# Four stores instead of two for the last 64 tokens of each sequence, in a gated recurrence with soft MoE slots

## The chip, the cores and the metric

The kernel runs on one core of a Trainium2 chip. The metric is the device time of one execution in microseconds; the median of the runs counts.

## The reference, cut to what matters

```python
B, S, D = 4, 5056, 256
# 1. a gated recurrence over each sequence
f = lower_bound + (1 - lower_bound) * sigmoid(f_logit)
for t in range(S):
    h = f[:, t] * h + (1 - f[:, t]) * x[:, t]
    y[:, t] = h
x = y.reshape(B * S, D)                    # 20224 tokens
# 2. soft MoE: 8 experts with 4 slots each, 32 slots
logits = x @ phi
d = softmax(logits, over all tokens)
slot_input = (d.T @ x).reshape(8, 4, D)
for e in range(8):
    slot_out[e] = relu(slot_input[e] @ w1[e]) @ w2[e]
c = softmax(logits, over the 32 slots)
out = c @ slot_out.reshape(32, D)          # 20224 x 256, float32
```

Every token's output needs the slots' outputs, and these need every token. So no output row can be written before the whole input has been read and the experts are done.

## The kernel before, in words

The kernel has three stages on one core. The order on each engine is written out by hand.

Until about 118 us it reads `x` and `f_logit` in groups of 512 tokens of a sequence, forms the gates, turns them to channels by TensorE, runs the recurrence as a scan on VectorE (L319), and takes logits and exponentials from its result. The exponentials of all tokens stay in SBUF (`etall`; for the last L = 64 tokens of each sequence a copy in `left`). The weights of the experts come in meanwhile by GpSimd's DMA queue (`load_w`). Then follows the small expert stage (L605 to L749), in which the outputs of the slots are made.

The last stage begins near 143.5 us and writes 20.7 MB. For a tile of 128 rows, TensorE multiplies the exponentials with the slots' outputs, and VectorE (`by_vector`, L756) or ScalarE (`by_scalar`, L760) scales the rows from PSUM into a tile of the pool `osb`, which holds three buffers for each of the names `ob` and `oc`. SP (SyncE) issues every store, in this order:

- `early` (L747): two stores of 128 KB, the first rows of sequence 3.
- `pieces` (L796): five stores of 256 or 512 KB, the rest of the first 2048 tokens of sequence 3.
- `couple(end, 0)` and `couple(end, 1)` (L828): four stores of 896 KB, the tokens 4096 to 4991 of all four sequences.
- `rest` (L845): the last 64 tokens of all sequences. Its tile `ob` has on its 128 partitions 64 tokens x 2 sequences (partition 2t + u is token t of sequence 2j + u) and the two pairs j of sequences side by side. For each pair one store goes from 128 partitions with 1 KB each to `dst[64 tokens, 2 sequences]`, so every row is a run of 1 KB in DRAM.
- `whole` (L813): one store of 2 MB.
- three calls of `couple` (L828): six stores of 2 MB.

SP takes its instructions in order. Before a store it waits for the engines that fill the tile, and for the completion semaphore that this store will use. The program has eight such semaphores for SP's DMAs and uses them in turn, so that each store waits for the landing of the DMA eight places before it. After the last store SP waits for the landing of all (L882).

Of the kernel before, what the change touches and what calls it, by code (L numbers as in the profile page):

```python
# [18 lines left out]
def kernel(  # L19
# [10 lines left out]
    nc = tc.nc  # L30
    B, S, D = x.shape
# [17 lines left out]
    def used(g):  # L49
        return first(g + 1) - first(g) if g < n_grp - 1 else G  # L50
# [6 lines left out]
    L = used(odd) - P * R3  # L57
# [110 lines left out]
    with tc.tile_pool(name="sp2", bufs=3) as sp2, \  # L168
# [85 lines left out]
        def to_channels(n, ps, t, rest):  # L254
            t = t.bitcast(F32)
            if n // B == odd:
                flat = ps.rearrange("c p r -> c (p r)")
                sides = ident_f.rearrange("p (t u) -> p u t", u=2)
                v = flat[:, ds(0, P * R3)].rearrange("c (p r) -> c p r", r=R3)
                k = P * R3 - n % 2 * L  # L260
                nc.tensor.matmul(flat[:, ds(k, P)], rest.bitcast(F32), sides,
                                 is_transpose=True, start=True, stop=True)
                for r in range(R3):
                    nc.tensor.transpose(v[:, :, r], t[:, r], ident_f)
                return
            for r in range(R):
                nc.tensor.transpose(ps[:, :, r], t[:, r], ident_f)  # L267
# [337 lines left out]
    with tc.tile_pool(name="ew", bufs=1) as ew, \  # L605
# [36 lines left out]
        for q in range(E // Q):  # L642
# [4 lines left out]
            if q == 0:  # L647
                nc.tensor.matmul(cs_ps, rep2, cs1, start=True, stop=True)
            k = Q if q == 0 else Q - 1
# [4 lines left out]
            dst = hid[:, :, q * Q, ds(s0, SPE)]  # L654
            dst = bass.AP(tensor=dst.tensor, offset=dst.offset,
                          ap=[list(dst.ap[0]), [(E - 1) * NS, FC], [NS + SPE, k], [1, SPE]])
# [55 lines left out]
        for i in range(len(blocks)):  # L712
            expert(Q + i)
            row_sums(i)
            if i < len(blocks) - 1:
                k = ds(i * wide_r, wide_r)
# [3 lines left out]
        k = len(blocks) - 1  # L720
# [32 lines left out]
    with tc.tile_pool(name="osb", bufs=3, reuse_waits="tile") as osb:  # L753

        def by_vector(ob, op, scale):
            nc.vector.tensor_tensor(ob, op, scale.broadcast_to(list(ob.shape)), ALU.mult)  # L756
# [22 lines left out]
        def bank():  # L779
            return pout.tile([P, 2, D], F32, name="op", tag="op")  # L780
# [49 lines left out]
        def rest():  # L830
            n_p = B // 2
            ob = osb.tile([P, n_p, D], F32, name="ob", tag="ob")
            dst = out.rearrange("(b t) d -> t b d", b=B)
            for j in range(n_p):
                k = ds(j * 2 * NS, 2 * NS)
                op = bank()
                nc.tensor.matmul(op.rearrange("p u d -> p (u d)"),
                                 left[k].rearrange("s t u -> s (t u)"),
                                 slot_bd[k].rearrange("s u d -> s (u d)"),
                                 start=True, stop=True, skip_group_check=True)  # L840
                nc.scalar.copy(ob[:, j], op[:, 0])
                nc.vector.tensor_tensor(ob[:, j], ob[:, j], op[:, 1], ALU.add)
            by_vector(ob, ob, rrow[:, n_grp * R - 1, ds(0, n_p)].unsqueeze(2))
            for j in range(n_p):
                nc.sync.dma_start(out=dst[ds(S - L, L), ds(2 * j, 2)], in_=ob[:, j])  # L845

        pieces(0, B - 1)
        end = len(blocks) - 1
        couple(end, 0)
        couple(end, 1)  # L850
        rest()
        whole(0, B - 2)
        for i in range(end):
# [33 lines left out]
```

## Time and profile before

| what | value |
|---|---|
| median of 3 runs | 198.1 us (197.61 to 198.96) |
| profiled execution | 197.64 us, of which the span is 195.9 us |
| PE, DVE, ACT, POOL busy, share of the span | 76%, 73%, 73%, 52% |
| HBM read and written | 58.23 MB and 20.71 MB |
| DMA packets | 14161, of them 2866 under 2 KB |
| last stage | 143.5 us to the end |

The span runs from the first to the last instruction on the core; the profiled execution's own time has 1.7 us more around it. Engine shares are averages over stages with different limits: in the last 20 us no compute engine works, and stores alone are under way. A DMA of this kernel is cut into packets, one for each row, which 16 DMA engines of the core work off, and each engine sends a mark of 4 bytes when its share of a store is done. Where a time "to landing" is given, it runs from the issue on SP to the last of these marks.

### The profile page before, as it was taken

The page shows a single profiled execution, that of the slowest core. Times are in us where ns is not written, and L with a number is a line of the kernel's source. Part 1 is how long each engine was busy: PE and PEld are TensorE (multiplying, and loading weights), DVE is VectorE, ACT ScalarE, POOL GpSimd, SP SyncE. Part 2 cuts the span into 40 slices and gives each one's busy share as a digit, 9 for nine tenths or more (in the row PEclk, how much of TensorE's full clock was granted, in tenths as well). Part 3 has the DMA queues.
Part 4 walks back from the last instruction along what each step waited for, and adds up shares of the span by engine and source line. Part 5 has one row for each costly group of instructions (what it writes and reads, how often), then busy time and mean ns, then how long its engine had stood idle before and what let it go on. Part 6 is the DMA issues. An engine that isn't in the chain of part 4 may idle for free.

```text
span 195.9 us, 3272 instructions
## 1 busy us (share of the span) xinstructions
PE 149.7 (76%) x1204; PEld 105.0 (54%) x1204; DVE 143.9 (73%) x185; ACT 142.0 (73%) x200; POOL 101.2 (52%) x78
## 2 busy tenths in 40 slices
PE   0687599977998979899797988997899999930000
PEld 0465468675776767767585856556674434300000
DVE  2669859989799999999999999543377998930000
ACT  3689686899889999999987799434089999950000
POOL 2589578774998688874969979280030000000000
PEclk9999759996999999999999999999996555555555
DMA  5999999999999999999999999999849999999994
GB/s 195 416 419 421 433 428 423 428 428 363 363 422 428 412 331 427 423 414 333 379 420 421 253 218 213 213 212 214 162 170 424 429 424 428 425 445 435 445 435 174
DMA packets 14161, 70.75 MB, mean 361 GB/s; under 512 B 1585, under 2 KB 2866, under 8 KB 10178
## 3 DMA queue, kind: packets, MB, share of 16 engines
q1 hardware_dynamic: 11520, 62.13, 76.5%
q0 software_dynamic: 2624, 8.42, 21.6%
q8 instruction: 9, 0.15, 0.3%
q14 instruction: 6, 0.05, 0.1%
q10 hardware_dynamic: 2, 0.00, 0.0%
HBM read 58.23 MB, written 20.71 MB: 403 GB/s over the span
## 4 chain that ended last, share of the span: by engine, by line
PE 34%; DMA 24%; DVE 13%; POOL 9%; issue 5%; ACT 4%; ACTq 0%; SPq 0%; POOLq 0%
DMA x_t<-in_x_dram 14%; DVE h L319 10%; DMA w_t<-in_moe_w_dram 9%; PE op L822 9%; POOL u_t L252 7%; PE hp L332 5%; PE up L273 4%; PE sp L267 4%; ACT oc L760 3%; DVE ht L351 3%; PE op L766 3%; PE slot_ps L189 2%; PE lg L365 2%; POOL w_sb L147 2%; PE slot_ps L416 1%
## 5 line engine op out<-in xcount | busy, mean ns | idle before, releaser
L252 POOL TENSOR_TENSOR u_t<-s_t,x_t 128x1024 bf16<-128x1024 bf16 (+1 forms) x39 | 82.5, 2131 | 22.6 <-ACT s_t L241 11.8
L319 DVE TENSOR_TENSOR_SCAN h<-a,h,up 128x512 bf16<-128x512 f32 (+1 forms) x72 | 86.8, 1253 | 4.5 <-PE up L273 2.2
L241 ACT ACTIVATE s_t<-f_t 128x2048 bf16<-128x2048 f32 (+2 forms) x23 | 38.3, 1668 | 4.9 <-DMA f_t<-in_f_logit_dram 4.9
L332 PE MATMUL hp<-ident_f,h 128*128 128x128 f32 (+1 forms) x160 | 29.4, 308 | 7.9 <-DVE ht L351 6.7
L332 PEld LDWEIGHTS hp<-ident_f,h 128*128 128x128 f32 (+1 forms) x160 | 23.5, 207 | 19.1 <-DVE ht L351 12.6
L267 PE MATMUL sp<-ident_f,s_t 128*128 128x128 f32 x144 | 22.1, 298 | 6.9 <-ACT s_t L241 4.6
L301 ACT ACTIVATE a<-sp,lbs 128x1024 f32<-128x1024 bf16 x24 | 25.4, 1114 | 1.1 <-PE sp L267 0.6
L760 ACT ACTIVATE oc<-op,rrow 128x256 f32<-128x256 f32 x62 | 24.5, 513 | 0.2
L822 PE MATMUL op<-slot_bd,etall 64*128 64x512 bf16 x62 | 23.3, 582 | 0.5 <-ACT oc L760 0.3
L267 PEld LDWEIGHTS sp<-ident_f,s_t 128*128 128x128 f32 x144 | 18.0, 155 | 8.7 <-ACT s_t L241 5.1
L756 DVE TENSOR_TENSOR oc<-op,rrow 128x512 f32<-128x512 f32 x31 | 19.9, 686 | 1.9 <-PE op L822 1.8
L308 ACT ACTIVATE a<-sp,lbs 128x512 f32<-128x512 bf16 (+2 forms) x22 | 17.8, 858 | 4.7 <-PE sp L267 4.3
L273 PE MATMUL up<-ident_f,u_t 64*128 64x64 f32 x192 | 17.8, 231 | 1.8 <-POOL u_t L252 1.8
L189 PE MATMUL slot_ps<-rep,ident_f 128*128 128x256 f32 x52 | 17.5, 432 | 0.0
L273 PEld LDWEIGHTS up<-ident_f,u_t 64*128 64x128 f32 x192 | 14.1, 139 | 5.6 <-POOL u_t L252 2.1
L822 PEld LDWEIGHTS <-etall 64*128 64x128 bf16 x62 | 9.1, 154 | 13.4 <-issue 7.9
L351 ACT COPY ht<-hp 128x512 f32<-128x512 f32 (+1 forms) x20 | 11.6, 582 | 5.3 <-PE hp L332 5.2
L351 DVE COPY ht<-hp 128x512 f32<-128x512 f32 (+1 forms) x20 | 13.4, 669 | 1.3 <-PE hp L332 1.3
L319 DVE TENSOR_TENSOR_SCAN h<-a,up 128x512 bf16<-128x512 f32 x8 | 9.3, 1208 | 2.5 <-ACT a L308 1.6
L365 PE MATMUL lg<-h,phi 128*32 128x512 bf16 (+1 forms) x80 | 9.8, 412 | 0.3 <-ACT et L389 0.2
L267 PE MATMUL up<-ident_f,u_t 128*128 128x128 f32 x48 | 9.4, 328 | 0.6 <-POOL u_t L252 0.6
L189 PEld LDWEIGHTS slot_ps<-rep,ident_f 128*128 128x128 f32 x52 | 8.5, 199 | 1.8 <-issue 0.8
(127 smaller groups left out, 144.1 us busy)
## 6 DMA issues: line engine op xcount, KB each, us to landing
f_t<-in_f_logit_dram SPq DMA_DIRECT2D x12, 1024.0 KB, 12.1
x_t<-in_x_dram SPq DMA_DIRECT2D x12, 1024.0 KB, 11.5
out_dram<-oc SPq DMA_DIRECT2D x6, 2048.0 KB, 13.4
w_sb<-in_moe_w_dram POOLq DMA_DIRECT2D x14, 512.0 KB, 10.3
f_t<-in_f_logit_dram SPq DMA_DIRECT2D x12, 512.0 KB, 8.4
x_t<-in_x_dram SPq DMA_DIRECT2D x12, 512.0 KB, 9.9
out_dram<-oc SPq DMA_DIRECT2D x4, 896.0 KB, 6.1
out_dram<-ob SPq DMA_DIRECT2D x1, 2048.0 KB, 9.3
```

What stands on the lines that cost most here:

```text
L189: nc.tensor.matmul(slot_bank[:, 1], ident_f, wide_rep, start=False, stop=False, skip_group_check=True)
L241: nc.scalar.activation(s_t, f_t, ACT.Sigmoid, scale=-1.0)
L252: nc.gpsimd.tensor_tensor(uts[n][:, :r], s_t[:, :r], x_t[:, :r], ALU.mult)
L267: nc.tensor.transpose(ps[:, :, r], t[:, r], ident_f)
L273: nc.tensor.transpose(v[:, :, r], t(r)[k].bitcast(F32), ident_f[k, k])
L301: nc.scalar.activation(a, sp[:, :, :, :, o], ACT.Identity, scale=nomlb[:, ds(o, 1)], bias=1.0)
L319: nc.vector.tensor_tensor_scan(h[:, :T, o], decays[n // 2, o][:, n % 2, :T], up[:, :T, o], hs[number(g - 1, b)][:, ds(used(g - 1) - 1, 1), ...
L332: nc.tensor.transpose(hp[:n_p, r], hw[:, :n_p, r], ident_f)
L351: copy(hts[g][:n_p, b].rearrange("p r d -> p (r d)").bitcast(F32), hps.pop(n)[:n_p].rearrange("p r c -> p (r c)"))
L756: nc.vector.tensor_tensor(ob, op, scale.broadcast_to(list(ob.shape)), ALU.mult)
L760: nc.scalar.activation(ob[:, i], op[:, i], ACT.Copy, scale=scale[:, i])
L822: nc.tensor.matmul(op.rearrange("p u d -> p (u d)"), ew[:, :, r], slot_bd[ds(j * 2 * NS, 2 * NS)].rearrange("s u d -> s (u d)"), start=Tru ...
```

## The change

Each of the two stores of `rest` becomes two: one of the first 60 tokens (120 partitions) and one of the last 4 tokens (8 partitions). The bytes, the tile and the places in DRAM are the same, and no other instruction changes; SP issues 4 DMAs there instead of 2, and the stores behind them take the next completion semaphores but two.

```diff
             for j in range(n_p):
-                nc.sync.dma_start(out=dst[ds(S - L, L), ds(2 * j, 2)], in_=ob[:, j])
+                for t, k in ((0, L - 4), (L - 4, 4)):
+                    nc.sync.dma_start(out=dst[ds(S - L + t, k), ds(2 * j, 2)],
+                                      in_=ob[ds(2 * t, 2 * k), j])
```

## The prediction

> **What bounds the kernel now.** I read the page's slices first, then the windows of the last 50 us, then what SP (the engine that issues every store here) waits for, then its timeline, and last the packets of single stretches. The slices (40 of 4.9 us each):
>
> ```profile
> DMA  5999999999999999999999999999849999999994
> GB/s 195 416 419 421 433 428 423 428 428 363 363 422 428 412 331 427 423 414 333 379 420 421 253 218 213 213 212 214 162 170 424 429 424 428 425 445 435 445 435 174
> ```
>
> The stores run from slice 31 (147 us) to the last one at 424 to 445 GB/s, as fast as the loads ever went. The changed stores, L845, lie in slice 32. The windows say whether a compute engine is behind that:
>
> ```profile
> 150.00:158.00 8.00, 7.97 (x29) 4.21 (x28) 6.71 (x13) 7.99 (x23) 0.00 (x0) 0.50 1.01 423
> ...
> 174.00:192.00 18.00, 0.00 (x0) 0.00 (x0) 0.00 (x0) 0.26 (x1) 0.00 (x0) 0.50 0.99 422
> ```
>
> The columns are the stretch, its length, the busy time of PE, PEld, DVE, ACT and POOL, the granted clock, the DMA share and GB/s. After 174 us nothing computes, and the DMA engines are full (0.99) for 18 us more. SP's own waits say the same:
>
> ```profile
> SPq L882 <- DMA out_dram<-oc: 18.9, 1, 18.9
> SPq L828 <- DVE oc L756: 14.8, 5, 5.0
> ```
>
> The last store is issued at 175.5 us and SP then stands 18.9 us for landings. So the end is set by bytes on the DMA engines. A change counts only if it gives the most loaded DMA engine more time, or lets the queue run dry between 145 and 193 us.
>
> Packets show that the 16 DMA engines do not end together. The stretch 193.3 to 194.2 us:
>
> ```profile
> DMA packets 13, 0.03 MB, mean 36 GB/s; under 512 B 11, under 2 KB 11, under 8 KB 11
> q1 hardware_dynamic: 13, 0.03, 9.2%
> ```
>
> Eleven are completion marks; only two are data, 16 KB each. 9.2% of 16 engines x 0.9 us is 1.32 us, so a 16 KB packet takes about 0.6 us. Nearly all engines finish their data around 193.3; two still start a packet then and end near 194.0. The two late engines decide the end, and the rest have some 0.6 us to spare.
>
> **The change, part by part.** Four stores take the place of two. Bytes stay the same, and so do the packets: dst rows are 1 KB each, 128 a store, 256 in all before and (120 + 8) x 2 = 256 after. PE, DVE, ACT and POOL run the same instructions in the same order. The tile of L845 is in no buffer that is written again, so nobody but the end waits for its landings. What moves is how the rows fall on the 16 engines, and how long SP is at it.
>
> *Rows on engines.* The price of a row comes from 144.0 to 145.3 us, when the `early` rows of 1 KB went out:
>
> ```profile
> DMA packets 276, 0.26 MB, mean 199 GB/s; under 512 B 24, under 2 KB 276, under 8 KB 276
> q1 hardware_dynamic: 276, 0.26, 59.9%
> ```
>
> 59.9% of 16 x 1.3 us is 12.5 us; over 252 data packets (and 24 small marks) that is at most 49 ns each; I take 46, as the marks take a part. Before, 256 rows on 16 engines are 16 each, 0.74 us of every engine. After, the new stores carry 120 and 8 rows. No store in this trace has such a count. The nearest rows: stores of 128 rows, which go out at the full rate of all engines (424 GB/s), and at the far end the one-row load, one data packet and its mark on a single engine:
>
> ```profile
> q10 hardware_dynamic: 2, 0.00, 0.0%
> ```
>
> Even spread is the one end: 16 or 17 rows on the busiest engine, 0 to +0.05 us. All on one engine is the other: 256 rows, (256 - 16) x 46 ns = 11.0 us more there, and the end moves by 10.4 to 11.0 as that engine has 0.6 us to spare or not. 120 rows are far nearer 128 than 1, so I take a nearly even spread, in which the 8 rows of a short store lie on a few engines: with two more rows there per pair, 4 x 46 ns = 0.18 us. If these engines are not the two late ones, their 0.6 us hides it; if one is, the end moves by 0.18. I take +0.1 us.
>
> [...]
>
> *SP.* Its timeline around the change (start, us, what):
>
> ```profile
> 153.38 2.19 SPq L845 DMA_DIRECT2D out_dram<-ob  x2
> 155.81 1.18 SPq L813 DMA_DIRECT2D out_dram<-ob  x1
> 161.25 14.29 SPq L828 DMA_DIRECT2D out_dram<-oc  x6
> ```
>
> The two old stores of L845 (ns shortest, middle, longest, and when they were issued):
>
> ```profile
> L845 SPq DMA_DIRECT2D out_dram<-ob x2: 744/1066/1389, 153.4 to 154.2; - x2
> ```
>
> Two more issues cost from 2 x (332 + 46) ns = 0.8 us (the shortest DMA issue of L828, with the gap to the next) to 2 x (1389 + 46) = 2.9 us (the longer one of L845). I take L845's middle, 1.07 + 0.05 each, 2.2 us. Behind them on SP stands the 2 MB store of whole() (L813), which moves from 155.8 to about 158.0 (bounds 156.6 and 158.7). After it come the stores of L828; the first waits for DVE (5.0 us at the longest, until 161.25), and L813 done at 158.0 + 1.18 = 159.2, or 159.9 at worst, is before that. So the six last stores keep their times, and only L813 can leave the queue dry.
>
> The DMA issues (KB each, us from issue to landing) give the queue ahead of it:
>
> ```profile
> out_dram<-ob SPq DMA_DIRECT2D x1, 2048.0 KB, 9.3
> ...
> out_dram<-early SPq DMA_DIRECT2D x2, 128.0 KB, 1.8
> out_dram<-ob SPq DMA_DIRECT2D x2, 128.0 KB, 6.1
> ```
>
> From issue to landing L813 took 9.3 us. Its own bytes need 2.097 MB / 422 GB/s = 5.0; the `early` store with an empty queue took 1.8, of which 8 rows x 46 ns = 0.4 are data, so 1.4 are fixed. 9.3 - 5.0 - 1.4 = 2.9 us of queue lay ahead of it on the late engines, and 2.9 - 0.6 = 2.3 on the others. A delay of 2.2 fits under both. At 2.9 the 14 engines run dry for 0.6 us, which is what they have to spare, and the late ones just do not. Price: 0, bounds 0 and +0.6.
>
> *Semaphores.* SP's DMAs take eight completion semaphores in turn, each waiting for the landing of the one eight before. Two more stores shift this by two: L813 now waits for the first 896 KB store (issued 148.9, landed at the least 4.3 us later by L828's row, 153.2) instead of a store of L796; the next ones wait for the other 896 KB stores, which lie ahead of the old L845 pair in the queue, and that pair had landed at 154.2 + 6.1 = 160.3, before 161.25. Cost 0; if that cover were gone, the queue left at 161.25 (L813 lands at 165.1) would pay first.
>
> *Sum.* 0.1 (rows) + 0 (SP) + 0 (semaphores). The profiled execution, 195.9 us of span in 197.64, becomes 196.0 and 197.7. It lay 0.46 under the median of the three runs, 198.1, so the median becomes 198.2.
>
> **The rivals.**
>
> *One engine carries the rows of a 60-token store* (slower). Point of decision: an engine with n rows ends (n - 16) x 46 ns later, less 0.6 of spare, so the end moves by 1% (2 us) from n = 60 to 73 on, which is 120 rows a pair on four engines or fewer. On one engine 208.5 to 209; on four, (64 - 16) x 46 ns = 2.2, less up to 0.6: 199.7 to 200.3. For it: a count that is no multiple of 16 is unseen here, and the one-row load did stay on one engine. Against: 120 rows can be dealt out as 8 each to 15.
>
> *The queue runs dry before L813* (slower, by little). If all four issues run at the slow 1.4 us and the first bytes come late, the end moves by up to 0.6: 198.7. It would need an issue of over 3 us each to make 1%.
>
> *Each store's fixed 1.4 us is paid in line.* Two more stores would add 2.8 us: 200.9. [...] Against it in the trace: five stores of L796 were issued 0.4 us apart and the window 146 to 148 us still had a DMA share of 1.07; fixed parts overlapped.
>
> *Faster.* If the engine that gets no rows of the 60-token stores is the last of the two late ones, the other one decides, about 0.1 us earlier: 198.0. [...] No mechanism here gives 1%: the bytes are the same and the last store is issued when compute is done.
>
> **How the numbers follow.** Forecast (with the 0.1 either way) 0.68; dry queue 0.10; fixed cost in line 0.05; rows on four engines 0.07; on one 0.07; clearly faster by something not seen 0.03. About 1%, 2 us, can be told from no change here. Slower by more: one engine 0.07, fixed cost 0.05, half of the four-engine case 0.04, and 0.02 for spread of the runs (197.6 to 199.0): 0.18. Faster by more: 0.03. Same: 0.79. The range must hold 198.2 with the spread of the runs, 198.7, and the four-engine case: 197.3 to 200.3. It leaves out one engine, fixed cost and part of faster, some 0.15.
>
> **What would show it.** Right: the packets under 2 KB keep their number but for the marks; DMA share stays at 0.99 or more from 146 to 193 us; L813's issue moves to 156.6 to 158.7 and its landing time falls by as much; the first L828 of the last six stays at 161.25 within its own spread; the last landing stays within 0.2 us. Wrong: after the stretch where 14 engines end, 1 KB packets or more than two late engines are left over; a slice under 400 GB/s around 159 us; or a wait of SP for a landing ahead of L813.

## The result, and the profile after

The changed kernel takes 198.73 us in the median of 20 runs (198.49 to 200.62), the kernel before 197.61 us in 20 runs of its own (197.41 to 198.96). The ratio is 1.0053, 95% interval 1.0038 to 1.0067: about 1.05 us slower (the two medians lie 1.12 us apart). That lies inside the range of the prediction and under the 1% from which on it counts a change, but it is ten times the 0.1 us of its sum. The profiled execution of the changed kernel has a span of 197.1 us in 198.83.

The page's slices of the changed kernel (4.9 us each):

```profile
DMA  5999999999999999999999999999669999999993
GB/s 203 419 421 420 427 429 424 429 426 383 353 426 426 421 318 426 422 415 343 369 420 416 232 211 213 214 214 213 124 239 430 429 370 432 429 429 429 426 426 166
```

Slice 33 (157.7 to 162.6 us) moved 370 GB/s where the kernel before had 424. SP's timeline of the changed kernel (start, us, what) shows one step that was mis-sized:

```profile
153.41 5.65 SPq L846 DMA_DIRECT2D out_dram<-ob  x4
159.17 0.37 SPq L813 DMA_DIRECT2D out_dram<-ob  x1
161.50 1.62 SPq L828 DMA_DIRECT2D out_dram<-oc  x2
```

The four stores hold SP for 5.65 us, and `whole`'s 2 MB store (L813) goes out at 159.17, 3.36 us later than before. The windows of the changed kernel (stretch, length, busy PE, PEld, DVE, ACT, POOL, clock, DMA share, GB/s):

```profile
158.00:159.00 1.00, 1.00 (x3) 0.33 (x2) 0.90 (x3) 0.99 (x4) 0.00 (x0) 0.50 0.92 307
159.00:160.00 1.00, 1.00 (x4) 0.42 (x3) 0.84 (x2) 0.99 (x3) 0.00 (x0) 0.50 0.60 185
```

The same stretches of the kernel before:

```profile
158.00:159.00 1.00, 1.00 (x4) 0.44 (x3) 1.00 (x3) 0.99 (x3) 0.00 (x0) 0.50 1.01 391
159.00:160.00 1.00, 1.00 (x4) 0.33 (x2) 0.86 (x2) 0.97 (x4) 0.00 (x0) 0.50 1.50 613
```

A packet counts where it starts, so a share can pass 1. Between 159 and 160 us the queue did run dry on most engines: at 159.8 us only 3 of the 16 have a packet under way. That would be a complete story, but it does not set the end. The packets after 194.4 us in the changed kernel:

```profile
DMA packets 2, 0.02 MB, mean 14 GB/s; under 512 B 1, under 2 KB 1, under 8 KB 1
```

One engine alone has a 16 KB packet to go when all others are done. In the packet records the other 15 end their data at 194.12 to 194.38, this one at 195.54 (before: 193.3 to 193.4, and the two late ones at 193.97 and 194.07). If the dry stretch were all, the end would be near 194.4, only 0.3 later than before. The one late engine decides, and it did not run dry there: between its last 7 KB packets it stood still for no more than 0.05 us at a time. Instead its 7 KB packets became slow. The packets that start between 159.1 and 160 us, first of the changed kernel:

```profile
DMA packets 167, 0.16 MB, mean 173 GB/s; under 512 B 27, under 2 KB 165, under 8 KB 167
```

and of the kernel before:

```profile
DMA packets 133, 0.58 MB, mean 642 GB/s; under 512 B 19, under 2 KB 103, under 8 KB 103
```

Between "under 2 KB" and "under 8 KB" lie the 7 KB packets of the stores ahead. Before, none starts after 159.1. After, two do: they took 696 and 740 ns where 272 is the rule, after one of 586. A window of 0.01 us around the start of such a packet shows its length, since a packet counts whole where it starts. The window 158.545 to 158.555 us, then 159.88 to 159.89:

```profile
q1 hardware_dynamic: 1, 0.01, 366.2%
```

```profile
q1 hardware_dynamic: 1, 0.01, 462.5%
```

366.2% of 16 engines x 0.01 us is 586 ns, and 462.5% is 740. That engine landed its share of the last 896 KB store at 160.97, against 159.58 before: 1.39 us of loss ahead of any row of the changed stores on it. Four other engines had a slow 7 KB packet, too (445 to 614 ns, from 158.33 us on), but these have time to spare.

### The profile page after: what moved, and what is told of

The parts are those of the page before. It is cut to its first block, busy times and chain, and to the rows that moved or that the text cites. A ratio compares the mean times of both kernels' runs of the same rounds, so it can differ in the third digit from the quotient of the medians.

```text
span 197.1 us, 3274 instructions
## 1 busy us (share of the span) xinstructions
PE 150.2 (76%) x1204; PEld 105.1 (53%) x1204; DVE 144.2 (73%) x185; ACT 142.3 (72%) x200; POOL 101.4 (51%) x78
## 4 chain that ended last, share of the span: by engine, by line
PE 26%; DMA 23%; DVE 15%; POOL 9%; ACT 9%; issue 5%; ACTq 0%; SPq 0%; POOLq 0%
DMA x_t<-in_x_dram 14%; DVE h L319 12%; PE op L822 9%; DMA w_t<-in_moe_w_dram 9%; POOL u_t L252 7%; ACT oc L760 3%; PE hp L332 3%; DVE ht L351 3%; PE up L273 3%; PE op L766 3%; PE sp L267 2%; ACT s_t L241 2%; POOL w_sb L147 2%; PE lg L365 1%; PE slot_ps L189 1%
## 5 line engine op out<-in xcount | busy, mean ns | idle before, releaser
L332 PE MATMUL hp<-ident_f,h 128*128 128x128 f32 (+1 forms) x160 | 29.9, 313 | 9.5 <-DVE ht L351 8.2
```

Of the source, the lines that this page charges most:

```text
L332: nc.tensor.transpose(hp[:n_p, r], hw[:, :n_p, r], ident_f)
```

## The experiments

Three theories. A: SP is late with `whole`, and the queue runs dry. B: 15 and 4 engines in place of 16 load the rows unevenly. C (formed after the first four runs): with less than 128 partitions in a store, rows leave SBUF through other engines than those that serve these partitions in the full stores, and so slow down an engine that is still at its 7 KB rows. C is a guess: no trace names the engine or the partition of a packet. "Late engine" is the last mark of the last 896 KB store, "end" the last mark of all, both from the profiled execution; each ratio is to runs of the kernel before taken beside that kernel.

| kernel | whole() issued, us | late engine, us | end, us | ratio to before (95%) |
|---|---|---|---|---|
| before | 155.81 | 159.58 | 194.54 | 1 |
| changed | 159.17 | 160.97 | 195.85 | 1.0053 (1.0038 to 1.0067) |
| e1, 32 + 32 tokens | 158.61 | 160.53 | 195.22 | 1.0016 (0.9997 to 1.0035) |
| e2, behind whole() | 155.65 | 159.43 | 195.42 | 1.0044 (1.0018 to 1.0069) |
| e3, the 60 alone | 155.87 | 160.20 | 195.23 | 1.0034 (1.0012 to 1.0056) |
| e4, 61 + 3 | 165.55 | 161.50 | 205.04 | 1.0519 (1.0484 to 1.0554) |
| e5, column halves | 158.25 | 159.50 | 194.55 | 0.9996 (0.9988 to 1.0005) |
| e6, tokens 32 to 63 alone | 155.87 | 159.63 | 194.39 | 0.9999 (0.9986 to 1.0011) |
| e7, tokens 0 to 31 alone | 155.73 | 160.20 | 194.96 | 1.0026 (1.0014 to 1.0037) |
| e8, changed again | 159.08 | 160.91 | 195.80 | 1.0056 (1.0044 to 1.0068) |
| e9, six column stores | 159.62 | 159.58 | 195.43 | 1.0038 (1.0024 to 1.0052) |
| e10, eight column stores | 161.01 | 159.69 | 196.78 | 1.0093 (1.0079 to 1.0107) |

**e1: even halves.**

```diff
-                for t, k in ((0, L - 4), (L - 4, 4)):
+                for t, k in ((0, 32), (32, 32)):
```

> Theory A (late issue): the four issues of L846 hold SP, whole()'s 2 MB store is issued 3.4 us late as in the changed kernel, and the queue runs dry near 159.3 us. Four stores of 32 tokens cost SP about as much, so A expects +0.8 to +1.2 us over the kernel before, whole() issued near 159 us and the DMA share of 159 to 160 us near 0.6. Theory B (uneven rows): the stores of 60 tokens run on 15 DMA engines and those of 4 on four, one of the late engines among them, and its 7 KB packets grow from 272 to 586 to 740 ns. With 64 rows a store on all 16 engines B expects no slow 7 KB packets, the last engine where it was before, and -0.1 to +0.3 us.

Neither theory fits. SP is as late as A says (158.61), but the medians differ by 0.48 us (198.16 against 197.68 us; the interval of the ratio, 0.9997 to 1.0035, just includes no loss) and not by 0.8 to 1.2, and the late engine again has slow 7 KB packets (533 and 853 ns) although all 16 engines share the rows, against B.

**e2: the same stores behind whole().** Here `rest` hands its stores back instead of issuing them (that part of the edit is left out below).

```diff
-        rest()
+        stores = rest()
         whole(0, B - 2)
+        stores()
```

> The same 60 and 4 token stores, issued behind whole()'s store instead of ahead of it. A: whole() is issued near 155.7 us, its bytes fill the queue while SP is at the four stores, no dry stretch, -0.2 to +0.3 us against the kernel before. B: the same rows lie on the same engines, so the four rows more on one late engine and the slow packets stay: +0.6 to +1.2 us.

`whole` goes out at 155.65, ahead of the changed stores, and the loss stays (198.45 us). That speaks against A as the cause. The slow packets moved too: now 16 KB packets of `whole` are slow, nine of them, with 684 to 1047 ns (611 is the rule), at 162.7 to 164.7 us, about when the 1 KB rows run beside them. Two of them, of 895 and 1047 ns, follow each other; 0.72 us over the rule and the 0.18 us of the added rows make 0.90, and the end moved by 0.88.

**e3: the 4-token stores left out.**

```diff
-                for t, k in ((0, L - 4), (L - 4, 4)):
+                for t, k in ((0, L - 4),):
```

> Only the two stores of 60 tokens are issued; the last 4 tokens of each sequence are left unwritten. SP has two issues as before. A: whole() is issued at 155.8 to 156.5 us, no dry stretch, -0.2 to +0.3 us. B: if the 15-engine spread makes the slow packets, they stay (+0.6 to +1.0 us); if the four-engine stores make them, they go.

SP's timeline of this kernel:

```profile
153.30 2.46 SPq L846 DMA_DIRECT2D out_dram<-ob  x2
155.87 1.29 SPq L813 DMA_DIRECT2D out_dram<-ob  x1
```

SP is as before, there is no late issue, and 0.64 us are lost (198.32 against 197.68). So the stores of 60 tokens alone make more than half of the loss, without A. The late engine is 0.62 us later at its last 896 KB mark, which is nearly the whole of it.

**e4: a prime number of tokens.**

```diff
-                for t, k in ((0, L - 4), (L - 4, 4)):
+                for t, k in ((0, L - 3), (L - 3, 3)):
```

> The split is 61 and 3 tokens. If the number of engines is the largest up to 16 that divides both 61 and 122, a 61-token store has all its 122 rows of 1 KB on one engine: 244 + 4 rows there against 16, 232 x 46 ns = 10.7 us more, less 0 to 0.7 us of spare: +10 to +10.7 us. If rows are dealt out to all engines whatever their number, +0.8 to +1.2 us as with 60 and 4.

207.93 us, 10.25 more than 197.68: the 61-token stores do run on one engine. The issues of L846 (ns shortest, middle, longest) show SP standing behind it, too:

```profile
L846 SPq DMA_DIRECT2D out_dram<-ob x4: 667/2977/5312, 153.3 to 160.3; - x4
```

The number of engines can be read from the page, because each engine that takes part in a store sends one mark: the packet records of the kernel before have 1280 marks for SP's 80 DMAs, 16 each, so the two stores of 128 rows bring 2 x 16. The line of the kernel before, of the changed kernel, of e3, of e4 and of e1:

```profile
q1 hardware_dynamic: 11520, 62.13, 76.5%
```

```profile
q1 hardware_dynamic: 11526, 62.13, 76.1%
```

```profile
q1 hardware_dynamic: 11502, 62.12, 76.4%
```

```profile
q1 hardware_dynamic: 11496, 62.13, 72.8%
```

```profile
q1 hardware_dynamic: 11552, 62.13, 76.5%
```

The 6 more of the changed kernel are 2 x (15 + 4) - 32. e3 has 18 less: 16 rows, and 2 marks, which are 2 x 15 - 32. The 24 less of e4 are 2 x (1 + 3) - 32; another split of the 4 would give the same count, but not 10.25 us. The 32 more of e1 are 4 x 16 - 32. So these runs had 16 engines for 64 and for 32 tokens, 15 for 60, 4 for 4, 3 for 3 and 1 for 61: each time the largest number up to 16 that divides the tokens. Other counts were not tried.

**e5: columns, not tokens.** Four stores again, but each with all 128 partitions.

```diff
-                for t, k in ((0, L - 4), (L - 4, 4)):
-                    nc.sync.dma_start(out=dst[ds(S - L + t, k), ds(2 * j, 2)],
-                                      in_=ob[ds(2 * t, 2 * k), j])
+                for c in range(0, D, D // 2):
+                    nc.sync.dma_start(
+                        out=dst[ds(S - L, L), ds(2 * j, 2), ds(c, D // 2)],
+                        in_=ob[:, j, ds(c, D // 2)])
```

> Four stores as in the change, but each of all 64 tokens (128 partitions) and half of the columns, 512 rows of 512 B. Theory A (late issue): SP is as long at them, whole() is issued near 158.7 us, the queue runs dry for some tenths, and the time is +0.5 to +1.1 us over the kernel before. Theory C (crossed rows): the late engine's packets get slow because, with less than 128 partitions in a store, rows go out through other engines than those that serve the same partitions in the 128-partition stores, so that two engines draw on the same part of SBUF. Here all 128 partitions are in each store: no packet of 7168 B over 400 ns near 159 us, the last engine lands its 896 KB share where it did before (159.6 us), and the time is 0 to +0.4 us, the latter for the smaller rows.

SP's timeline of e5, and its windows:

```profile
153.30 4.84 SPq L846 DMA_DIRECT2D out_dram<-ob  x4
158.25 0.67 SPq L813 DMA_DIRECT2D out_dram<-ob  x1
```

```profile
158.00:159.00 1.00, 1.00 (x4) 0.41 (x3) 1.00 (x3) 1.00 (x4) 0.00 (x0) 0.50 0.95 332
159.00:160.00 1.00, 1.00 (x3) 0.33 (x2) 0.99 (x3) 0.99 (x4) 0.00 (x0) 0.50 1.02 379
```

Four issues, `whole` 2.4 us late, twice the packets: and no loss, 197.53 against 197.58 us. No 7 KB packet in the stretch is over 400 ns. The queue runs dry here, too, but for less time: at 159.4 us only two engines have a packet under way. Splitting these stores in four by columns, each with all partitions, costs nothing.

**e6 and e7: one half of the partitions.** Both have two stores, 64 rows each, on 16 engines (by the marks of e1), and leave the other 32 tokens unwritten. The two edits are shown as one:

```diff
-                for t, k in ((0, L - 4), (L - 4, 4)):
+                for t, k in ((32, 32),):        # e6
+                for t, k in ((0, 32),):         # e7
```

> Only the tokens 32 to 63 of the last 64 are stored (partitions 64 to 127), in two stores; the other 32 tokens are left unwritten. To be read beside its twin with the tokens 0 to 31. [...] Theory B (uneven rows): both halves are spread evenly on 16 engines, so both kernels take the same time, -0.5 to 0.

> The twin: only the tokens 0 to 31 are stored (partitions 0 to 63), the other 32 are left unwritten. [...] Theory B: the same time as the twin.

SP's last wait in e6, then in e7:

```profile
SPq L884 <- DMA out_dram<-oc: 18.7, 1, 18.7
```

```profile
SPq L884 <- DMA out_dram<-oc: 19.3, 1, 19.3
```

The upper half costs nothing (197.46 us), the lower half 0.45 (198.03 against 197.58). In e7 the late engine had a 7 KB packet of 609 ns right after one of 487; in e6 two packets took 415 and 422 ns, and the late engine's mark stands at 159.63, as before. Number of stores, issues, engines and rows are the same. What differs is which partitions the rows leave from (and which tokens they are; but e5 writes all of these tokens without loss). By B the two would have taken the same time. So C is shown as far as this: these rows from partitions 0 to 63, taken by all 16 engines, slow the late engine (0.45 us lost), and those from 64 to 127 do not (197.46 against 197.58 us).

What the rows share with the late engine's packets no run here shows. Crowding by many engines is not the whole of it: in e4 hardly more than one other engine had a packet under way from 158.9 to 161.1 us (the DMA share from 159 to 160 is 0.15), the one with the 61-token rows, and still the late engine's last two 7 KB packets took 1021 and 1352 ns.

**e8: the changed kernel again.**

> The changed kernel once more, beside these. Both theories: +0.9 to +1.2 us over the kernel before. If the slow 7 KB packets of one engine set the end they are here again, at the same place (158.4 to 160.6 us) and to the same sum (1.2 to 1.5 us); if they were an accident of the one profiled execution, they are not, and the time must come from the dry stretch.

198.72 us, and the same slow packets in the same place: 598, 702 and 759 ns, 1.24 us over three times 272. They are no accident of one execution.

**e9 and e10: when a late issue does cost.** The loop of e5 with other widths of columns:

```diff
-                for c in range(0, D, D // 2):
+                for c, w in ((0, 128), (128, 64), (192, 64)):                  # e9
+                for c, w in ((0, 64), (64, 64), (128, 64), (192, 64)):         # e10
```

> Six stores in the place of the change's four, each of all 64 tokens (128 partitions), with 128, 64 and 64 of the 256 columns. Theory C (crossed rows) has nothing to act on. What is asked is from which delay on a late issue of whole() costs: four such stores issued it 2.4 us late at no cost. Two more at 1.43 us each make that 5.3 us, near 161.1 us. Its first bytes come some 1.0 us later; the late engine ends its rows near 160.3 and the others near 159.8, so the late engine stands dry for about 1.8 us: +1.5 to +2.2 us. If late issues are always hidden, 0 to +0.3 us.

> Eight stores of all 64 tokens and 64 columns each. whole() is issued 8.2 us late, near 164.0 us, and the six last stores behind it wait too: the late engine stands dry for about 4.6 us, +4.2 to +5.2 us over the kernel before. If late issues are always hidden, 0 to +0.5 us.

Timeline of SP and a window of e10:

```profile
153.46 7.44 SPq L846 DMA_DIRECT2D out_dram<-ob  x8
161.01 0.52 SPq L813 DMA_DIRECT2D out_dram<-ob  x1
```

```profile
160.00:161.00 1.00, 1.00 (x3) 0.32 (x2) 0.84 (x2) 0.99 (x3) 0.00 (x0) 0.50 0.20 44
```

The time was +0.72 us (198.31) with `whole` at 159.62 and +1.86 us (199.45) at 161.01; with e5, nothing at 158.25. My expectations were too high, because I let each further issue take 1.43 us: once the DMA engines have run dry an issue takes 0.60 us (the eight of e10 took 7.44 us, the six of e9 6.14), so SP catches up. The step from e9 to e10 is 1.14 us for 1.39 us of delay; drawn back at that slope, a late issue behind stores of all 128 partitions begins to cost near 158.7. At 159.17, where the changed kernel has it, that would be some 0.35 us (an estimate from these two points), close to the 0.3 by which the last of its 15 other engines ends after the old end. The shorter rows of e9 and e10 do not explain the loss: all 16 engines stand idle just before `whole`'s first packets (160.5 and 162.0 us). The two losses do not add: the end is the later of the two, and that is the late engine.

## Why the prediction was right or wrong

**What bounds the kernel** was right: bytes on the DMA engines, and of these the last engine. The runs in which this engine's packets kept their length and the queue stayed full enough (e5, e6) left the time alone (ratios 0.9996 and 0.9999).

**Rows on engines** is the step that failed. The nearly even spread was right, though no run of before showed that 8 rows would lie on four engines: by the marks it is 15 and 4 engines, the busiest with 4 rows more, and one of the four is the late engine: its packet records after 160.63 us show 8, 2, 8 and 2 rows, each group closed by a mark. So the 0.18 us is paid. But the sum priced a row at 46 ns on its own engine and nothing on any other. It took for granted that it costs nothing which partitions the rows leave from; e7 and e6, which differ in that, are 0.57 us apart. The three slow packets add 586 + 696 + 740 - 3 x 272 = 1.2 us to the late engine, and they were in none of the terms. With the 0.18 that is 1.4, near the 1.31 by which the end moved (194.54 to 195.85). What these three packets share with the rows beside them stays open.

**SP** was sized too low. I took 2.2 us for the two added issues, with 2.9 as the upper bound; it was 3.36, for the four took 1050 to 1917 ns each, one longer than any of SP's in the trace before (1389). So the queue did run dry, on 13 engines, on most of them for 0.4 to 0.8 us. That this costs little on its own was right, for the reason given: those engines have about 0.6 us to spare, and they end no more than 0.3 us after the old end.

**Semaphores** were right: L813 had to wait for no landing; the last of the four issues ended at 159.06, L813 went out at 159.17.

**The rivals.** One engine for a 60-token store did not happen, but e4 bears out its pricing: 10.25 us for the 244 rows of the two 61-token stores on one engine, (244 - 16) x 46 ns = 10.5 less up to 0.6 of spare, where the prediction had 10.4 to 11.0 for all 256. The dry queue happened without being the cause; its price of up to 0.6 was of the right size. The fixed cost paid in line did not happen: e5 has the same number of stores at no cost. The faster case did not either: the late engine took 8 rows of each 60-token store, so it was not the relieved one. By the marks of e4 it is one of the three that take the 3-token stores, and not the one with the 61-token rows. Why it is the late one no run shows.

Its own signs told this apart: `whole` went out at 159.17, behind the 158.7 that was the bound, a slice near 159 us fell under 400 GB/s (370), and the last landing moved by 1.31 us and not 0.2. So the forecast held by luck, because all bounded terms are small against 198 us, and not because its sum was right: 0.1 us was predicted, by a term of 0.18, and 1.05 were found, from a mechanism that the prediction does not name.

## What to carry to other kernels

When stores bound the end, look for the last DMA engine, not at the mean share: a visible dry stretch on 13 engines was hidden here behind slow packets on one engine, and these cost a microsecond. Keep all 128 partitions in each store, and if a store must be split, split its columns: e5 did so in halves at no cost where 60 + 4 tokens lost 1.05 us. Finer cuts lost 0.72 and 1.86 us by the late issue behind them (e9, e10). The split into 61 + 3 tokens, with all 61-token rows on one engine, is worse by far: it lost 10.25 us on a quarter of a megabyte.

## What the runs showed of the hardware that I had not expected

- A packet can take several times as long while another engine's rows from part of the partitions run beside it: 7 KB up to 853 ns (e1) and 1352 ns (e4) in place of 272, 16 KB up to 1047 ns in place of 611 (e2), 1 KB up to 187 ns in place of 46 (e3).
- The time that SP spends on one issue varies widely: 1.05 to 1.92 us for the four stores in a row of the changed kernel, 0.60 us once the engines were dry (e10), and 5.3 us behind a store that sits on one engine (e4). Busy engines alone do not make it long: in e2 `whole` took 0.33 us with the engines full (DMA share 1.02 from 150 to 158 us), 2.9 us after SP's last issue. What sets it was not tried.
- One engine's marks come late in each of these kernels already ahead of the changed stores: in the kernel before, the last mark of the second 256 KB store of `pieces` came at 147.63, the others by 147.30, and of the third at 148.60 against 148.02. Why this engine is held up there was not tried.
